# Last 64 tokens as one high|low operand, a 256-key first score tile, and a moved weight split

## The chip, the cores and the metric

The kernel runs on one core of one Trainium2 chip. The metric is the device time of one execution in microseconds; the kernel before takes 835.9 us, the median of 3 runs (834.54 to 836.42). Five engines work in parallel: TensorE (PE, matmuls; PEld is its loading of the stationary operand), VectorE (DVE), ScalarE (ACT), GpSimd (POOL) and SyncE (SP, which issues DMAs here).

## What is computed

For each of 8 batches of 576 tokens and 8 heads of 64:

```python
def sm_attn(qq, kk, vv):                       # softmax attention
    ...
p_packed = sm_attn(p, k, v)                    # 32 packed queries
out = sm_attn(q, p_packed, p_packed)           # 576 tokens over 32 packed keys
...
h = gelu_tanh(x @ w_in)                        # 512 -> 1024
u, v = h[..., :512], h[..., 512:]
v_n = (v - mu) / sqrt(var + 1e-06) * g_ln      # norm over 512 features
v_s = einsum('ts,bsd->btd', w_sg, v_n) + b_sg  # mixing of tokens
x = x + (u * v_s) @ w_out
...
logits = x @ w_gate                            # 4 experts, the best 2 weighted by softmax
for e in range(E):                             # causal attention of head size 64 each
    ye = causal_attn(x @ wq[e], x @ wk[e], x @ wv[e]) @ wo[e]
    out += weight[e] * ye
```

## The kernel before

**Precision.** Each float32 product is three matmuls of a reduced-precision format (fp32r): every operand is split in a high part and a low part (the remainder), and the passes are high·high, high·low and low·high (`PASSES`; names end in h and l, as gh, gl, a2h, a2l, vnh, vnl). ScalarE usually makes the high part by a copy into fp32r, and VectorE or POOL the low part by a subtraction.

**Tokens.** 576 tokens are five tiles, 4 of 128 and one of 64 (`TOK`, tile c = 4). `VT` groups them as (0,1), (2,3), (4,). Operands that are stationary for tile 4 have 128 columns in v (a2 is stored 640 wide, with its last 64 columns repeated) and 64 columns in vlog.

**One batch b.** (1) Packed attention: pp, the 32 packed keys and values; s (L392), the tokens' scores against them, turned into weights bt and a2f; their split a2h/a2l (`a2_split`). (2) W' = ppT·w_in (wp, L605), copied and split into wph (ScalarE, L621) and wpl (VectorE, L85). (3) `front`: v = a2·W' (`v_mm`, L667), gelu (`v_gelu`, L672), norm (`v_stats` L677 to L681, `v_pow` on POOL, `v_scale` L689, `v_high` L695 and L697 on ScalarE, `v_low` L704 to L708 on VectorE), which gives vnh and vnl of each token tile; u in four tiles of 128 features (`u_tile`, L748). (4) vs = w_sg·vn in four column tiles m (`vs_mm`, L778 for token tiles 0 to 3 in order, six matmuls each, then L782 and L784 for tile 4); the gate g = u·vs and its split (`gate_high`, `gate_low`). (5) qk (L834 from the gate, L846 from the packed attention) and vlog (L877, L881), which makes the values v2 and the 4 gate logits lg; `gates` makes the expert weights. (6) Causal attention of the batch, by steps with one letter and a number: S, the scores sc of a query tile j (0 to 4) and a head pair pr, with mask, maximum nm, exp and sums (`att_exp`, L930 to L940; where matmuls are named apart they are S and the rest E; number 2j + pr, so E1 is query tile 0, pair 1, and E3 query tile 1, pair 1); N, the division by the sums (L946 to L949); T, transposes; y and o, values and output product.

**Order.** TensorE and SP run in the order of the program's text. The attention of batch b, the packed attention of batch b+1 and the transposing loads of batch b+2 (kx and qx, by DMA through DRAM copies turned_k and turned_q, one step per `tick`) are interleaved by hand, in `later_back` and `back`; batch 0's start has a written order (`ORDER`). The order on VectorE, ScalarE and POOL is laid down by a scheduler when the program is built, apart from stretches marked `manual_schedule`. So a change of the text can move steps of these engines far from it.

**w_o.** `prep_w_o` (L347) loads each half of the output weight (wst, by SP), makes its high part on ScalarE (L82) and its low part on POOL (L85). It is called at the end of `first_back`, ahead of the first steps of batch 2.

**PSUM.** Products go to one tag of four buffers (`pd`); the slots of tag A in SBUF hold the gate's parts, two column tiles in one slot of 1152.

## Time and profile before

| | |
|---|---|
| Median of 3 runs | 835.9 us (834.54 to 836.42) |
| The profiled execution | 836.55 us, its span 834.8 us |
| Mean granted TensorE clock | 0.994 |
| TensorE busy | 802.2 us, 96%, 7523 matmuls |
| VectorE busy | 571.7 us, 68% |
| ScalarE busy | 429.1 us, 51% |
| POOL busy | 228.0 us, 27% |
| Chain that ended last | TensorE 81%, VectorE 8%, DMA 6%, ScalarE 2% |

The span is the time from the first to the last recorded instruction; the execution's own time is a little longer. The chain is followed back from the last instruction, at each step to what released it. A matmul's duration in the trace is its time through the array, and matmuls overlap: the pace of a row of them is read from their starts. Times are in us from the span's start. In brackets behind a row of a timeline stands the engine's idle time before it and what ended it. The step from batch to batch is 94.1 us in the middle of the span.

### The profile page before, as it was taken

To read this page: it belongs to the slowest core of one execution; us is meant where nothing else is said; L and a number is where in the kernel's file an instruction comes from. 1 tells how busy PE (TensorE), PEld (TensorE's weight loads), DVE (VectorE), ACT (ScalarE), POOL (GpSimd) and SP (SyncE) were. 2 spreads that over 40 slices of the span, in tenths; PEclk is the share of its full clock that TensorE was granted. 3 is DMA by queue.
4 is the path that set the end of the run, shared out by engine and by line. 5 is a ranking of instruction groups with operands and counts; after the bars stand their busy time and mean duration, and the time that the engine had idled before them with its cause. 6 is when DMAs were issued, how large, how long until landed. Compare 5 with 4: busy or idle time off the path is not lost.

```text
span 834.8 us, 19249 instructions
## 1 busy us (share of the span) xinstructions
PE 802.2 (96%) x7523; PEld 693.3 (83%) x7523; DVE 571.7 (68%) x1359; ACT 429.1 (51%) x983; POOL 228.0 (27%) x301
## 2 busy tenths in 40 slices
...
GB/s 253 288 186 170 230 268 133 174 50 220 147 154 108 107 224 113 177 43 222 142 163 107 103 227 113 161 58 217 147 155 116 98 232 8 77 14 27 20 2 58
DMA packets 172710, 115.00 MB, mean 138 GB/s; under 512 B 119306, under 2 KB 153610, under 8 KB 169804
## 3 DMA queue, kind: packets, MB, share of 16 engines
...
q10 hardware_dynamic: 6976, 1.58, 0.9%
...
HBM read 69.18 MB, written 29.63 MB: 118 GB/s over the span
## 4 chain that ended last, share of the span: by engine, by line
PE 81%; DVE 8%; DMA 6%; ACT 2%; issue 1%; SPq 1%; ACTq 0%; POOL 0%; DVEq 0%; POOLq 0%
PE vs L778 11%; PE qk L834 11%; PE y L1017 7%; PE vlog L877 6%; PE qk L846 6%; PE v L667 6%; PE u L748 5%; PE o L1066 5%; PE sc L930 4%; PE aTp L988 4%; PE vlog L881 3%; PE s L392 2%; PE sc L961 2%; PE aTp L1002 1%; DVE wpl L85 1%
## 5 line engine op out<-in xcount | busy, mean ns | idle before, releaser
L473 POOL COPY kT<-kp 128x576 uint16<-128x576 uint16 x56 | 50.8, 984 | 159.3 <-DMA kp<-turned_k 135.1
L778 PE MATMUL vs<-w_sg,vnh 128*128 128x288 f32 x512 | 91.6, 301 | 1.5 <-ACT vs L82 1.5
L834 PE MATMUL qk<-gh,w_qk 128*128 128x288 f32 x512 | 90.6, 299 | 0.0
L940 ACT ACTIVATE at<-sc,nm 128x256 f32<-128x256 f32 (+3 forms) x128 | 66.1, 525 | 37.9 <-DVE nm L934 34.3
L834 PEld LDWEIGHTS qk<-gh,w_qk 128*128 128x128 f32 x512 | 74.7, 188 | 9.7 <-issue 8.8
L778 PEld LDWEIGHTS vs<-w_sg,vnh 128*128 128x128 f32 x512 | 74.5, 188 | 8.3 <-issue 3.9
L82 ACT ACTIVATE aT<-aTp 128x512 f32<-128x512 f32 (+4 forms) x160 | 59.3, 437 | 18.4 <-PE aTp L988 13.3
...
L685 POOL TENSOR_TENSOR rstd<-rstd,mhalf 128x1 f32<-128x1 f32 x40 | 36.5, 917 | 88.5 <-DVE rstd L681 88.0
L877 PE MATMUL vlog<-w_vg,gh 128*128 128x260 f32 (+1 forms) x320 | 60.5, 287 | 0.0
L473 POOL COPY qT<-qp 128x576 uint16<-128x576 uint16 x56 | 43.0, 837 | 59.8 <-DMA qp<-turned_q 59.6
L1017 PE MATMUL y<-aT,v 128*64 128x128 f32 (+2 forms) x960 | 58.3, 263 | 1.0 <-ACT aT L82 0.9
L1017 PEld LDWEIGHTS y<-aT,v 128*64 128x64 f32 (+1 forms) x960 | 46.8, 136 | 13.3 <-issue 5.8
L949 DVE TENSOR_SCALAR at<-at,sm,gw 128x256 f32<-128x256 f32 (+3 forms) x128 | 54.9, 471 | 1.6
L778 PE MATMUL vs<-w_sg,vnl 128*128 128x288 f32 x256 | 54.8, 296 | 0.9 <-POOL vnl L85 0.9
L834 PE MATMUL qk<-gl,w_qk 128*128 128x288 f32 x256 | 54.8, 296 | 0.5 <-DVE gl L85 0.5
L934 DVE TENSOR_REDUCE nm<-sc 128x2 f32<-128x256 f32 (+3 forms) x64 | 51.3, 820 | 1.2
L877 PEld LDWEIGHTS vlog<-w_vg,gh 128*128 128x128 f32 (+1 forms) x320 | 47.1, 178 | 4.0 <-DVE lg L886 2.8
L1066 PE MATMUL o<-w_o,y 128*128 128x512 f32 x186 | 50.0, 403 | 0.0
L846 PE MATMUL qk<-a2h,bdq 128*128 128x288 f32 x256 | 45.9, 301 | 0.0
L877 PE MATMUL vlog<-w_vg,gl 128*128 128x260 f32 (+1 forms) x160 | 45.1, 282 | 0.0
L988 PE MATMUL aTp<-ident,at 128*128 128x128 f32 x320 | 43.3, 274 | 0.0
...
## 6 DMA issues: line engine op xcount, KB each, us to landing
...
```

The costliest lines, as they stand in the source:

```text
L82: nc.scalar.activation(o, i, AF.Copy, scale=scale)
L473: nc.gpsimd.tensor_copy(w[:, i], t[:, i].rearrange("p h n -> p (h n)"))
L778: nc.tensor.matmul(pt[:, h, :], s["vn", c][x][:, cols], w_sg[y][:, c, hs(h)], start=(c, x, y) == (0, 0, 0), stop=False)
L834: nc.tensor.matmul(o[:, h, :], W["w_qk"][y][:, m, cols], s["g", m][x][:, hs(h)], start=first and (m, x, y) == (0, 0, 0), stop=not first an ...
L846: nc.tensor.matmul(o[:, h, :], s["bd", Q][y][:, cols], s["a2", Q][x][:, hs(h)], start=first and (Q, x, y) == (0, 0, 0), stop=not first and ...
L877: nc.tensor.matmul(pt[:n, ci, :260], s["g", m][x][:, c * P:c * P + n], W["w_vg"][y][:, m, :], start=(m, x, y) == (0, 0, 0), stop=False)
L934: nc.vector.tensor_reduce(nm, pt[:, :, :L], axis=AX.X, op=OP.max, negate=True)
L940: nc.scalar.activation(ats[e][:, :L], pt[:, e, :L], AF.Exp, bias=nm[:, e:e + 1], accum_out=sm[:, e:e + 1])
L949: nc.vector.tensor_scalar(ats[e][:, :L], ats[e][:, :L], sm[:, e:e + 1], s["w"][:, j, 2 * pr + e:2 * pr + e + 1], op0=OP.mult, op1=OP.mult)
L988: nc.tensor.transpose(pt[:, e, c * P:c * P + P], ats[e][:, c * P:c * P + P], ident)
L1017: nc.tensor.matmul(pt[64 * e:64 * e + 64, pr * w:pr * w + w], s["v2"][:m, c, col:col + D], s["aT", pr, e, j][c][:m, :], start=c == 0, stop ...
L1066: nc.tensor.matmul(pt, ys[:, pr, x, :], W["w_o"][y][:, pr, :], start=i == 0, stop=i == 5)
```

## The change

Four things are changed.

1. For the last 64 tokens, high and low parts lie side by side as one stationary operand of 128 columns: in a2h (whose columns 576 to 639 now hold the low part of the last 64), and in the gate, where each column tile has a slot of its own, [high 576 | copy of the low part's last 64 | low 576]; the copy is `gate_beside`, four POOL copies a batch. `v_mm` of tile 4 then has four matmuls (2 passes by 2 halves Q) in place of six, and `vlog` of tile 4 twelve in place of 18. Rows 64 to 127 of the product hold the low parts' contributions, which are added: in `v_gelu` by a ScalarE copy and a VectorE addition ahead of the gelu, in `vlog` by a copy and an addition each for v2 and lg, and POOL copies lg to the upper rows. The low·low product comes in with it. The norm of tile 4 works on 64 partitions.
2. `front` computes tile 4 first, then tiles 0, 1, then 2, 3.
3. The first score tile (query tile 0) multiplies with 256 keys in place of 128; the second 128 are not read.
4. `prep_w_o` moves from the end of `first_back` to `back(0)`, behind qk(b, 1), keep_last_q and a tick.

Also `cmp` and `eq` of the gates share the tag "rem". The diff, cut to its core:

```diff
-        for o, i0, n in ((0, 0, S), (S, 512, 64)):
-            act_copy(hi[:, o:o + n], f[:, i0:i0 + n])
-            lo_part(nc.gpsimd, lo[:, o:o + n], f[:, i0:i0 + n], hi[:, o:o + n])
+        act_copy(hi[:, :S], f)
+        lo_part(nc.gpsimd, lo[:, :S], f, hi[:, :S])
+        lo_part(nc.gpsimd, hi[:, S:], f[:, 512:], hi[:, 512:S])
...
     def v_mm(b, pt, c):
         s = ST[b]
         n = 0
+        if c == 4:
+            for y in range(2):
+                for Q in range(2):
+                    nc.tensor.matmul(pt, s["a2", Q][0][:, 512:640], wp_part(b, 1, y, Q), start=n == 0, stop=n == 3)
+                    n += 1
+            return
         for x, y in PASSES:
             for Q in range(2):
                 nc.tensor.matmul(pt, s["a2", Q][x][:, c * P:(c + 1) * P], wp_part(b, 1, y, Q), start=n == 0, stop=n == 5)
                 n += 1
 
     def v_gelu(b, pt, c):
-        vg = ST[b]["vg", c] = slot("t", w=512, name="vg")
+        vg = slot("t", w=512, name="vg")
+        if c == 4:
+            vg = vg[:64]
+            act_copy(vg, pt[64:])
+            nc.vector.tensor_tensor(vg, vg, pt[:64], op=OP.add)
+            pt = vg
+        ST[b]["vg", c] = vg
         nc.scalar.activation(vg, pt, AF.Gelu_apprx_tanh)
...
     def v_high(b, c):
         s = ST[b]
         hi, lo = s["vn", c] = (slot("B", F32R, 512, name="vnh"), slot("B", F32R, 512, name="vnl"))
         vg, rstd = s["vg", c], s["rstd", c]
-        nc.scalar.activation(hi, vg, AF.Copy, scale=rstd)
+        nc.scalar.activation(hi[:TOK[c]], vg, AF.Copy, scale=rstd)
         if c == 4:
-            nc.scalar.activation(lo[:64], vg[:64], AF.Copy, scale=rstd[:64])
+            nc.scalar.activation(lo[:64], vg, AF.Copy, scale=rstd)
...
     def v_low(b, c):
...
         else:
-            nc.vector.scalar_tensor_tensor(hi[64:P], vg[64:P], rstd[64:P], hi[64:P].bitcast(F32),
-                                           op0=OP.mult, op1=OP.subtract)
+            nc.vector.scalar_tensor_tensor(hi[64:], vg, rstd, hi[:64].bitcast(F32), op0=OP.mult, op1=OP.subtract)
             nc.vector.memset(lo[64:P].bitcast(F32), 1.0)
...
     def gate_high(b, m):
         s = ST[b]
-        if ("gt2", m // 2) not in s:
-            s["gt2", m // 2] = (slot("A", F32R, name="gh"), slot("A", F32R, name="gl"))
-        a = (m % 2) * S
-        s["g", m] = [t[:, a:a + S] for t in s["gt2", m // 2]]
+        t = s["gx", m] = slot("A", F32R, name="g")
+        s["g", m] = [t[:, :S], t[:, S + 64:]]
...
+    def gate_beside(b):
+        for m in range(4):
+            t = ST[b]["gx", m]
+            nc.gpsimd.tensor_copy(t[:, S:S + 64], t[:, 2 * S:])
...
         pt = pd("vlog")
         for ci, c in enumerate(cs):
+            if n < P:
+                i = 0
+                for y in range(2):
+                    for m in range(4):
+                        nc.tensor.matmul(pt[:, 0, :260], s["gx", m][:, 512:640], W["w_vg"][y][:, m, :], start=i == 0,
+                                         stop=False)
+                        i += 1
+                    for Q in range(2):
+                        nc.tensor.matmul(pt[:, 0, :260], s["a2", Q][0][:, 512:640], s["bdv", Q][y], start=False,
+                                         stop=(y, Q) == (1, 1))
+                continue
             for m in range(4):
                 for x, y in PASSES:
-                    nc.tensor.matmul(pt[:n, ci, :260], s["g", m][x][:, c * P:c * P + n], W["w_vg"][y][:, m, :],
+                    nc.tensor.matmul(pt[:, ci, :260], s["g", m][x][:, c * P:c * P + P], W["w_vg"][y][:, m, :],
                                      start=(m, x, y) == (0, 0, 0), stop=False)
             for Q in range(2):
                 for x, y in PASSES:
-                    nc.tensor.matmul(pt[:n, ci, :260], s["a2", Q][x][:, c * P:c * P + n], s["bdv", Q][y],
+                    nc.tensor.matmul(pt[:, ci, :260], s["a2", Q][x][:, c * P:c * P + P], s["bdv", Q][y],
                                      start=False, stop=(Q, x, y) == (1, 1, 0))
-        nc.scalar.activation(s["v2"][:n, cs[0]:cs[0] + k, :], pt[:n, :k, :256], AF.Copy)
-
-        for o in range(0, P, n):
-            nc.vector.tensor_copy(s["lg"][o:o + n, cs[0]:cs[0] + k, :], pt[:n, :k, 256:260])
+        if n < P:
+            v4, l4 = s["v2"][:n, 4, :], s["lg"][:, 4, :]
+            nc.scalar.activation(v4, pt[n:, 0, :256], AF.Copy)
+            nc.vector.tensor_tensor(v4, v4, pt[:n, 0, :256], op=OP.add)
+            nc.vector.tensor_copy(l4[:n], pt[n:, 0, 256:260])
+            nc.vector.tensor_tensor(l4[:n], l4[:n], pt[:n, 0, 256:260], op=OP.add)
+            nc.gpsimd.tensor_copy(l4[n:], l4[:n])
+            return
+        nc.scalar.activation(s["v2"][:, cs[0]:cs[0] + k, :], pt[:, :k, :256], AF.Copy)
+        nc.vector.tensor_copy(s["lg"][:, cs[0]:cs[0] + k, :], pt[:, :k, 256:260])
...
         L = j * P + P
+        n = max(L, 2 * P)
         qs, ks = s["qk", pr], s["qk", 2 + pr]
         pt = pd("sc")
         for i, (x, y) in enumerate(PASSES):
             for e in range(2):
                 r = slice(64 * e, 64 * e + 64)
-                nc.tensor.matmul(pt[:, e, :L], qs[x][r, j * P:L], ks[y][r, :L], start=i == 0, stop=i == 2)
+                nc.tensor.matmul(pt[:, e, :n], qs[x][r, j * P:L], ks[y][r, :n], start=i == 0, stop=i == 2)
         nc.vector.tensor_tensor(pt[:, :, j * P:L], pt[:, :, j * P:L],
...
     def front(b, go):
 
-        for cs in VT:
+        for cs in (VT[2], VT[0], VT[1]):
             v_tiles(b, cs)
             tick()
...
         keep_last_q(b, 0)
+        gate_beside(b)
         do_all("p0 Q0 p1 Q1")
         vlog(b, VT[2])
         do_all("P0 P1")
         vlog(b, VT[1])
         do_all("r")
-        for j in range(2):
-            prep_w_o(j)
         ahead(b + 2)
...
         qk(b, 1)
         keep_last_q(b, 1)
         tick()
+        if b == 0:
+            for j in range(2):
+                prep_w_o(j)
         nxt("E0 E2")
```

How the change moves instructions is shown at three places, with the operations as the built programs have them (the numbers behind a name tell buffers apart; line numbers after the change are those of the new file).

**ScalarE, from the front's last steps to the first exps of the attention, batch 1 (batches 2 to 7 read the same).** vnh is the high part of a token tile's normed v, 64x512 for tile 4, vnl 64x512 the high part's copy for its second operand; at<-sc is an exp. Before:

```order
L695 ACTIVATE vnh<-vg,rstd 128x512
L755 ACTIVATE u<-u 128x576
L695 ACTIVATE vnh<-vg,rstd 128x512
L755 ACTIVATE u<-u 128x576
L695 ACTIVATE vnh<-vg,rstd 128x512
L697 ACTIVATE vnl<-vg,rstd 64x512
L940 ACT_TABLE_LOAD
L940 ACTIVATE at,sm_2004<-sc,nm_2002 128x128 x2
L940 ACTIVATE at,sm_2022<-sc,nm_2020 128x256 x2
```

Now:

```order
L709 ACTIVATE vnh<-vg,rstd 128x512
L768 ACTIVATE u<-u 128x576
L709 ACTIVATE vnh<-vg,rstd 128x512
L684 ACTIVATE vg<-v 128x512
L768 ACTIVATE u<-u 128x576
L709 ACTIVATE vnh<-vg,rstd 128x512
L768 ACTIVATE u<-u 128x576
L973 ACT_TABLE_LOAD
L973 ACTIVATE at,sm_2000<-sc,nm_1998 128x128 x2
L709 ACTIVATE vnh<-vg,rstd 128x512
L973 ACTIVATE at,sm_2018<-sc,nm_2016 128x256 x2
```

Before, the five tiles' vnh all stand ahead of the table load. Now the last 128x512 vnh, that of tile 3, stands behind the load and the two exps of E1.

**VectorE, the same place.** causal is the mask's addition to a score tile, nm the row maximum (E1's first, then E3's), vnl<-vg,rstd,vnh a low part. Before:

```order
L681 TENSOR_SCALAR rstd<-mv 128x1
L689 SCALAR_TENSOR_TENSOR vg<-vg,mv,g_bc 128x512
L704 SCALAR_TENSOR_TENSOR vnl<-vg,rstd,vnh 128x512
L931 TENSOR_TENSOR sc<-sc,causal 128x2x128
L708 MEMSET vnl 64x512
L931 TENSOR_TENSOR sc<-sc,causal 128x2x128
L706 SCALAR_TENSOR_TENSOR vnh<-vg,rstd,vnh 64x512
L934 TENSOR_REDUCE nm_2002<-sc 128x2
L934 TENSOR_REDUCE nm_2020<-sc 128x2
L946 TENSOR_SCALAR sm_2004<-sm_2004 128x2
```

Now:

```order
L718 SCALAR_TENSOR_TENSOR vnl<-vg,rstd,vnh 128x512
L964 TENSOR_TENSOR sc<-sc,causal 128x2x128
L692 BN_AGGR mv<-bnst 128x2
L964 TENSOR_TENSOR sc<-sc,causal 128x2x128
L967 TENSOR_REDUCE nm_1998<-sc 128x2
L694 TENSOR_SCALAR rstd<-mv 128x1
L702 SCALAR_TENSOR_TENSOR vg<-vg,mv,g_bc 128x512
L967 TENSOR_REDUCE nm_2016<-sc 128x2
L979 TENSOR_SCALAR sm_2000<-sm_2000 128x2
L980 RECIPROCAL sm_2000<-sm_2000 128x2
L718 SCALAR_TENSOR_TENSOR vnl<-vg,rstd,vnh 128x512
L982 TENSOR_SCALAR at<-at,sm_2000,gw 128x128 x2
```

Before, both nm stand behind every step of the norm. Now rstd and scale of tile 3 stand between them, and its vnl behind both.

**SP, the end of batch 0.** Before:

```order
L196 DMA w_in_1338<-kept_in_110 128x2048
L351 DMA wst_1563<-in_moe_wo_dram 128x512
L351 DMA wst_1567<-in_moe_wo_dram 128x512
L438 DMA pn<-in_p_dram 128x2x64 x2
L455 DMA_TRANSPOSE kx<-in_k_dram 128x1152
L460 DMA turned_k_1682<-kx 128x1152
L455 DMA_TRANSPOSE kx<-in_k_dram 128x1152
```

Now:

```order
L196 DMA w_in_1336<-kept_in_110 128x2048
L438 DMA pn<-in_p_dram 128x2x64 x2
L455 DMA_TRANSPOSE kx<-in_k_dram 128x1152
L460 DMA turned_k_1668<-kx 128x1152
L455 DMA_TRANSPOSE kx<-in_k_dram 128x1152
L351 DMA wst_1674<-in_moe_wo_dram 128x512
L351 DMA wst_1678<-in_moe_wo_dram 128x512
L460 DMA turned_k_1723<-kx 128x1152
```

The two wst loads, w_o's halves, have moved behind pn, one kx, its turned_k and a second kx. On ScalarE, the split of w_o (L82) stood ahead of the copies of the first vlog (64x256), of ppT and of the second vlog. Now it stands behind them and ahead of the two bt exps; POOL has its low parts ahead of its bt steps before and now:

```order
L868 ACTIVATE qk<-qk 128x576
L912 ACTIVATE v_1431<-vlog 64x256
L426 ACTIVATE ppT<-ppT 128x128 x2
L918 ACTIVATE v_1431<-vlog 128x512
L82 ACTIVATE w_o_1672<-wst_1674 128x512
L82 ACTIVATE w_o_1672<-wst_1678 128x512
L527 ACTIVATE bt<-bt 128x576 x2
L918 ACTIVATE v_1431<-vlog 128x512
```

In this row of ScalarE only w_o's place has moved.

## Rows read from the trace of the kernel before

**Rows 1.** The page: span, and TensorE's busy time, share and instructions.

```profile
span 834.8 us, 19249 instructions
...
PE 802.2 (96%) x7523; PEld 693.3 (83%) x7523; DVE 571.7 (68%) x1359; ACT 429.1 (51%) x983; POOL 228.0 (27%) x301
```

**Rows 2.** The chain of waits, 330 to 362 us: start, us, what.

```profile
339.13 6.66 PE v L667 x28
...
352.47 0.89 PE sc L930 x12
353.36 3.38 PE vs L778 x24
```

**Rows 3.** The chain of waits, 400 to 425 us: vlog of tile 4, then of tiles 2, 3.

```profile
413.36 1.58 PE vlog L877 x12
...
415.65 1.45 PE vlog L877 x12
```

**Rows 4.** The instructions of vlog, 407 to 421 us: ns min/median/max, place, forms.

```profile
L877 PEld LDWEIGHTS vlog<-w_vg,gh x40: 133/188/192, 407.7 to 418.7; 128*128 128x128 f32 x32, 128*64 128x64 f32 x8
```

**Rows 5.** TensorE's groups by form, sc: count | busy us, mean ns | idle before.

```profile
L930 PE MATMUL sc<-qk 64*128 64x384 f32 x96 | 10.8, 353 | 0.0
L930 PE MATMUL sc<-qk 64*128 64x256 f32 x96 | 9.2, 297 | 0.7 <-ACT at L967 0.7
L930 PE MATMUL sc<-qk 64*128 64x128 f32 x96 | 8.8, 289 | 0.0
```

**Rows 6.** VectorE's timeline: start, us, operation [idle before <-releaser].

```profile
343.70 1.29 DVE L677 BATCH_NORM_STATS2 bnst<-vg 128x6 f32<-128x512 f32 x2 [1.45 <-ACT vg L672]
...
353.33 0.74 DVE L704 SCALAR_TENSOR_TENSOR vnl<-vg,rstd,vnh 128x512 fp32r<-128x512 f32 x1
353.99 0.42 DVE L931 TENSOR_TENSOR sc<-sc,causal 128x256 f32<-128x256 f32 x1
...
355.42 0.75 DVE L706 SCALAR_TENSOR_TENSOR vnh<-vg,rstd,vnh 64x512 fp32r<-64x512 f32 x1
356.20 1.02 DVE L934 TENSOR_REDUCE nm<-sc 128x2 f32<-128x256 f32 x2
```

**Rows 7.** ScalarE's timeline, the same place.

```profile
353.85 0.72 ACT L695 ACTIVATE vnh<-vg,rstd 128x512 fp32r<-128x512 f32 x1 [0.19 <-POOL rstd L685]
...
356.70 1.28 ACT L940 ACT_TABLE_LOAD   x1 [1.51 <-DVE nm L934]
358.00 0.37 ACT L940 ACTIVATE at<-sc,nm 128x128 f32<-128x128 f32 x1
```

**Rows 8.** SP's timeline, the end of batch 0.

```profile
117.38 2.57 SPq L196 DMA_DIRECT2D w_in<-kept_in  x2
...
124.09 5.12 SPq L455 DMA_TRANSPOSE kx<-in_k_dram  x1
132.14 0.36 SPq L460 DMA_DIRECT2D turned_k<-kx  x1
132.60 2.08 SPq L455 DMA_TRANSPOSE kx<-in_k_dram  x1
```

**Rows 9.** The chain of waits, 118 to 154 us.

```profile
122.34 8.26 DMA wst<-in_moe_wo_dram
```

**Rows 10.** POOL's timeline, the end of batch 0.

```profile
130.65 2.50 POOL L85 TENSOR_TENSOR w_o<-wst,w_o 128x512 fp32r<-128x512 f32 x2 [3.85 <-DMA wst<-in_moe_wo_dram]
134.50 1.16 POOL L526 TENSOR_TENSOR bt<-bt,mx 128x576 f32<-128x576 f32 x1 [1.36 <-DVE mx L525]
```

**Rows 11.** VectorE's timeline, the end of batch 0.

```profile
149.67 1.23 DVE L85 TENSOR_TENSOR wpl<-wp,wph 128x1024 fp32r<-128x1024 f32 x1 [2.36 <-ACT wph L621]
```

**Rows 12.** TensorE's timeline, the end of batch 0.

```profile
131.83 1.21 PE L392 MATMUL s<-qT,ppT 64*32 64x288 f32 x32 [1.83 <-ACT ppT L426]
```

**Rows 13.** Busy us (x) in stretches, PE PEld DVE ACT POOL, PEclk, DMA share, GB/s.

```profile
30.00:34.00 4.00, 1.28 (x22) 0.62 (x20) 3.93 (x7) 3.22 (x5) 1.27 (x1) 0.95 1.05 395
34.00:38.00 4.00, 3.61 (x5) 1.58 (x6) 3.40 (x7) 1.22 (x2) 1.03 (x1) 0.50 1.09 304
```

More of the change, by code (lines that the diff above doesn't have):

```diff
@@ L675, in v_stats @@
         s = ST[b]
-        st = small.tile([P, 6], F32, name="bnst")
+        n = TOK[c]
+        st = small.tile([P, 6], F32, name="bnst")[:n]
         nc.vector.bn_stats(st, s["vg", c])
-        mv = s["mv", c] = small.tile([P, 2], F32, name="mv")
+        mv = s["mv", c] = small.tile([P, 2], F32, name="mv")[:n]
         nc.vector.bn_aggr(mv, st)
-        rstd = s["rstd", c] = small.tile([P, 1], F32, name="rstd")
+        rstd = s["rstd", c] = small.tile([P, 1], F32, name="rstd")[:n]
         nc.vector.tensor_scalar(rstd, mv[:, 1:2], LN_EPS, None, op0=OP.add)
@@ L684, in v_pow @@
         rstd = ST[b]["rstd", c]
-        nc.gpsimd.tensor_tensor(rstd, rstd, mhalf, op=OP.pow)
+        nc.gpsimd.tensor_tensor(rstd, rstd, mhalf[:TOK[c]], op=OP.pow)
     def v_scale(b, c):
         s = ST[b]
-        nc.vector.scalar_tensor_tensor(s["vg", c], s["vg", c], s.pop(("mv", c))[:, 0:1], g_bc, op0=OP.subtract, op1=OP.mult)
+        nc.vector.scalar_tensor_tensor(s["vg", c], s["vg", c], s.pop(("mv", c))[:, 0:1], g_bc[:TOK[c]],
+                                       op0=OP.subtract, op1=OP.mult)
     def v_high(b, c):
@@ L714, in v_high_0 @@
         nc.scalar.activation(vg, vg, AF.Copy, scale=s.pop(("rstd", c)))
-        act_copy(hi, vg)
+        act_copy(hi[:TOK[c]], vg)
         if c == 4:
-            act_copy(lo[:64], vg[:64])
+            act_copy(lo[:64], vg)
     def v_low_0(b, c):
@@ L725, in v_low_0 @@
         else:
-            lo_part(nc.gpsimd, hi[64:P], vg[64:P], hi[64:P])
+            lo_part(nc.gpsimd, hi[64:], vg, hi[:64])
             nc.gpsimd.memset(lo[64:P].bitcast(F32), 1.0)
@@ L893, in gates @@
         mine = lg[:, :, :, None].to_broadcast(T4)
-        cmp = small.tile(T4, F32, name="cmp", bufs=1)
-        eq = small.tile(T4, F32, name="eq", bufs=1)
+        cmp, eq = [small.tile([P, 2 * D], F32, tag="rem", name=n, bufs=2)[:, :NT * E * E].rearrange("p (c i j) -> p c i j", c=NT, i=E) for n in ("cmp", "eq")]
         nc.vector.tensor_tensor(cmp, other, mine, op=OP.is_gt)
@@ L1170, in later_back @@
         keep_last_q(b, 0)
+        gate_beside(b)
         qk_gated(b, 2, True)
```

15 lines of the change are left out of this document (7 added, 8 removed).

## Prediction, made before the result was known

> **What bounds the kernel now.** I read the page first: TensorE is busy for 802.2 us of a span of 834.8 us [rows 1], so the end moves only by what changes TensorE's own work, or by waits that are put into its row. The profiled execution took 836.55 us; the sum below is made against that, and the median of the runs is 0.65 us lower. Next I read the chain of waits in a steady stretch. Batches repeat there, and between 339 and 361 us, which is the front of a batch, the chain is TensorE alone: v's matmuls from the third on, 28 in 6.66 us, u, 12 of sc (score tiles E1 and E3), then 24 of vs, the spatial gating's first column tile, in 3.38 us [rows 2]. So TensorE waits for nothing here, and a wait that appears here is paid in full, seven times, once for each of batches 1 to 7 (batch 0 has its own written order). Then I read what VectorE and ScalarE do in the same stretch, since they make what vs reads, and last the end of batch 0, which is where w_o's load is moved.
>
> **TensorE's work.** A v matmul takes 6.66/28 = 0.238 us [rows 2]; the last tile has 4 in place of 6, which saves 0.47 us. The last tile's vlog runs from 413.36 to the next tile's start at 415.65: 2.29 us for 18 matmuls. The next tile's 12 take 1.45 us with 128 stationary columns [rows 3], 0.121 each. Twelve of the wide kind in place of 18 narrow ones save at least 6 x 0.12 = 0.72 us and at most 2.29 - 1.45 = 0.84; I take 0.72, as the first matmuls of a tile also pay for the change of shape. That is 1.2 us a batch. The chance against it is the stationary load: 64 columns load in 133 ns and 128 in 188 ns [rows 4], so if the loads set the pace, 12 x 188 = 2.26 us against 18 x 133 = 2.39 us would save next to nothing. The steps of 0.121 and 0.127 us, both shorter than either load, say that loads run under the matmuls. The Trainium skill (TensorE: Matmul & The Clock Gate, section LDWEIGHTS) has the load's time proportional to its columns, 128/1.2 = 107 ns against 53; by it, as an estimate, 12 wide loads would take 1.28 us against 0.95, and vlog would lose time. The trace agrees on the direction, not on the ratio: 188 ns against 133.
>
> The first score tile gets 256 keys, 6 matmuls for each of 2 head pairs and 8 batches, 96 in all. By form, 128 keys take 289 ns and 256 take 297 [rows 5]: 96 x 8 ns = 0.8 us at most; two heads run beside each other, so half of that, 0.4. The upper end is the price of 128 more columns from 256 to 384, 353 - 297 = 56 ns, which is 2.7 us by the same halving. I take 0.4, whose rows are the very shapes.
>
> **The new order in front of vs.** ScalarE's order shows that the high part of tile 3 (vnh) now stands behind the exp table's load and the two exps of E1, and VectorE's order shows its rstd, scale and low part behind or between the row maxima. Before, all five tiles were finished ahead of the first maximum. When is tile 3 ready now?
> - VectorE begins its norm work at 343.70 and reaches E1's maximum (nm) at 356.20, almost without a pause [rows 6]. Two things bring that maximum forward. Tile 4 comes first: its four matmuls end some 1.4 us sooner than the first pair did, with a copy of about 0.6 us before its gelu, so the first statistics start about 1.1 us earlier (my estimate from the 0.46 us a pair of v matmuls takes). And tile 3's scale and low part (0.66 us each from start to start, as 353.33 to 353.99 [rows 6]), with its rstd, now come later: 1.4 us. So nm starts at about 356.20 - 1.1 - 1.4 = 353.7.
> - ScalarE waits for nm, loads the table at 356.70 and starts the first exp at 358.00 [rows 7]: 1.80 us behind nm's start. An exp of 128x128 takes 0.37 us [rows 7], two take 0.7. So 353.7 + 1.8 + 0.7 = 356.2 is where tile 3's vnh may begin; 0.72 us for it [rows 7], and it is there at 356.95.
> - TensorE starts vs at 353.36 - 0.47 (v is shorter), and reads tile 3 after 18 matmuls of 3.38/24 = 0.141 us: 352.9 + 2.5 = 355.4. It waits 1.55 us. Then the low part (0.74 us) is done at 357.7, and TensorE wants it 4 matmuls after 356.95, at 357.5: 0.2 more.
> - So 1.8 us a batch, 12.6 us over seven. The lower end: nm cannot start before E1's scores are there (half of the sc group's 0.89 us: 352.45) and both masks are added (0.40 each), some 353.3, which leaves 1.4; if the exps stood closer too, 0.9. The upper end: if norm operations of 64 partitions break the overlap of VectorE's steps (the 64-partition one starts 0.43 us after the mask before it [rows 6]) and nothing comes earlier, 2.5.
>
> ScalarE's two copies a batch (v and vlog of the last tile), VectorE's two adds, and POOL's four copies of low parts add about 1.2, 1.2 and 0.9 us. They stand where these engines wait for TensorE (ScalarE waits 1.51 us for nm alone [rows 7]); if that cover were gone, the cost would again be a wait of vs, and is inside the 2.5.
>
> **w_o's load, at the end of batch 0.** Before, its two DMAs go out on SP between w_in and the transposing load kx. They take 8.26 us to land [rows 9], and ScalarE's copy of them holds up ppT, for which TensorE waits 1.83 us before 131.83 [rows 12]. Moved, they stand on SP behind pn, kx, the store turned_k (which waits until kx has landed) and the next kx. Without them SP could go on from the end of w_in, 117.38 + 2.57 = 119.95; with the 1.2 us of pn between, the first kx goes out at 121.2 in place of 124.09, 2.9 us earlier. turned_k, before at 132.14, then comes at 129.3; the second kx takes 2.08 us [rows 8]; w_o goes out between 131.8 and 132.6. It lands 1.3 us later at best (133.9), 7.2 at worst (139.8, as slow as before); I take 136, since the big loads ahead of it (two w_in, one kx) have then landed. ScalarE's order has both halves of w_o ahead of the bt exps, and POOL's has its low parts (2.50 us for two) ahead of both bt steps [rows 10]. POOL's first bt step, before at 134.50, then starts at 136 + 0.7 + 2.5 = 139.2: 4.7 us later. From there a chain without gaps leads by bt, sums and a2f to the gates, E0's mask and exps, wph and wpl, which v of batch 1 needs. Its slack is the 2.36 us that VectorE waits before wpl [rows 11]. TensorE would lose about 2 to 3 us there, and with it what batch 0 saved (1.2) and the 1.8 us wait it no longer has before. Against the sum in which only batches 1 to 7 save, I put +3; the ends are -3 (landing at 133.9: the old wait and batch 0's saving are won) and +6.
>
> **The sum.** 7 x -1.2 = -8.4; score tile +0.4; vs +12.6; w_o +3: together +7.6 us, 844.1 for the profiled execution and 843.5 against the median. As the lower part of 0.9 to 2.5 is the better founded, I say **843.0**.
>
> **The rivals.**
> - *vs waits, w_o does not* (w_o lands by 134): -8.4 + 0.4 + 12.6 - 1.2 - 1.8 = +1.6, 837.5 against the median. For it: the 8.26 us were taken behind two w_in loads and beside kx. Against it: SP's own order, which cannot issue it before 131.8.
> - *The clock falls too.* A wait of some 4 us of TensorE before v of batch 1. Between 34 and 38 us, after a stretch in which TensorE was busy for 1.28 of 4 us, the granted clock is 0.50, its lower level of 1.2 GHz [rows 13]; that is some 1.7 us of work lost. With w_o at its upper end this is +7.6 + 3 + 1.7 = +12.3, about 848.
> - *w_o as forecast, no wait at vs*: -8.4 + 0.4 + 3 = -5.0, 831.
> - *The other side: faster.* Tile 3's parts are ready when vs wants them. The point that decides is E1's first maximum: if ScalarE is released by nm at 352.0 or before, vnh is done by 355.4. Then with w_o harmless the sum is -8.4 + 0.4 - 1.2 - 1.8 = -11, **825**. Against it: E1's scores are themselves only finished at about 352.47 + 0.45 - 0.47 = 352.45, and both masks go ahead of the maximum.
> - *Wide loads set the pace*, so that vlog saves nothing: 8 x 0.72 = 5.8 us more, 849. Against it: the steps of [rows 3]. The page named above speaks for it.
>
> **How the numbers follow.** My forecast, 839 to 846, has a chance of 0.48; vs alone (837.5) 0.16; the clock too (848) 0.12; w_o alone (831) 0.08; neither (825) 0.11; wide loads (849) 0.05. A measurement of this kernel tells about 0.2%, 1.7 us, from no change. Slower by more: 0.48 + 0.12 + 0.05 and a third of the second case, 0.70. Faster: 0.08 + 0.11 and a little of the second, 0.20. Same: 0.10. The range of 831 to 849 leaves out the case of 825, part of 831 and the end beyond 849, not quite 2 in 10. The likeliest one's own range is 839 to 846.
>
> **What would show it.** In the profile after: the vs matmuls of tile 3 with an idle time of 1 to 2 us put down to ScalarE's vnh, seven times; ScalarE's vnh right behind E1's exps; a v group that is 16 matmuls smaller and a vlog group 48 smaller, at unchanged steps; w_o's landing near 136 us and TensorE idle before v of batch 1; no more wait for ppT. If TensorE runs through tile 3 of vs without a pause, the forecast is wrong, and the time should be near 825 or 831.

## The result and the profile after

The changed kernel takes 845.6 us, the median of 4 runs (845.5 to 849.13), where before takes 835.22 (4 runs beside it): the ratio is 1.0135, with a 95% interval of 1.0103 to 1.0167. It is slower by 10.4 us of median. The profiled executions, 845.5 against 836.55 us, differ by 9.0 us, and so do their spans.

The page of the kernel after, against [rows 1]:

```profile
span 843.8 us, 19236 instructions
...
PE 800.4 (95%) x7459; PEld 689.2 (82%) x7459; DVE 568.9 (67%) x1375; ACT 431.4 (51%) x975; POOL 231.6 (27%) x341
```

TensorE has 64 fewer matmuls and is busy for 1.8 us less (its busy time holds the stretches at half clock that are read below), and the span is 9.0 us longer. The waits of TensorE say where that stands (what waited, on what: us in total, times, longest):

```profile
PE vs L791 <- ACT vnh L709: 11.4, 7, 1.6
...
PE qk L857 <- DVE lg L919: 2.3, 1, 2.3
```

Neither row exists before. The first is one wait in each of batches 1 to 7, the second stands at the end of batch 0. The three timelines of the batch that [rows 2, 6, 7] show (shifted by some 1.9 us, the distance that has added up until there) have the first wait in full. ScalarE:

```profile
352.37 0.59 ACT L684 ACTIVATE vg<-v 128x512 f32<-128x512 f32 x1
...
356.23 1.28 ACT L973 ACT_TABLE_LOAD   x1 [1.38 <-issue]
357.53 0.37 ACT L973 ACTIVATE at<-sc,nm 128x128 f32<-128x128 f32 x1
...
357.88 0.36 ACT L973 ACTIVATE at<-sc,nm 128x128 f32<-128x128 f32 x1
...
358.23 0.72 ACT L709 ACTIVATE vnh<-vg,rstd 128x512 fp32r<-128x512 f32 x1
```

VectorE:

```profile
344.40 0.69 DVE L690 BATCH_NORM_STATS2 bnst<-vg 64x6 f32<-64x512 f32 x1 [0.20 <-ACT vg L684]
...
349.47 0.48 DVE L721 MEMSET vnl<- 64x512 f32 x1 [0.16 <-issue]
...
353.73 0.69 DVE L690 BATCH_NORM_STATS2 bnst<-vg 128x6 f32<-128x512 f32 x1
...
355.01 0.43 DVE L964 TENSOR_TENSOR sc<-sc,causal 128x256 f32<-128x256 f32 x1
...
355.75 0.41 DVE L967 TENSOR_REDUCE nm<-sc 128x2 f32<-128x256 f32 x1
356.08 0.15 DVE L694 TENSOR_SCALAR rstd<-mv 128x1 f32<-128x1 f32 x1
356.14 0.74 DVE L702 SCALAR_TENSOR_TENSOR vg<-vg,mv,g_bc 128x512 f32<-128x512 f32 x1
...
358.98 0.75 DVE L718 SCALAR_TENSOR_TENSOR vnl<-vg,rstd,vnh 128x512 fp32r<-128x512 f32 x1 [0.24 <-ACT vnh L709]
```

TensorE:

```profile
354.73 0.79 PE L791 MATMUL vs<-w_sg,vnh 128*128 128x288 f32 x4
...
356.96 0.42 PE L791 MATMUL vs<-w_sg,vnl 128*128 128x288 f32 x2
359.00 0.79 PE L791 MATMUL vs<-w_sg,vnh 128*128 128x288 f32 x4 [1.62 <-ACT vnh L709]
359.78 0.53 PE L791 MATMUL vs<-w_sg,vnl 128*128 128x288 f32 x2
```

The reader follows it from row to row: tile 3's gelu stands on ScalarE at 352.37, its statistics on VectorE at 353.73; the masks are added from 355.01 on, E1's maximum is taken at 355.75, the table load follows at 356.23, the exps end at 358.23, and only then does ScalarE make tile 3's vnh. TensorE had come to it 1.62 us before 359.00. The low part starts at 358.98 and takes 0.75 us, so the pair that reads it starts 0.78 us after the four matmuls on vnh, where an undisturbed pair starts 0.53 after. The 1.62 us are counted from the end of the matmuls before; from start to start the pause is 1.78 us (356.96 to 359.00, less the 0.26 that an undisturbed pair takes).

The matmuls of both kernels come in the same groups, so each group's start can be set beside its twin's. In the shown batch the distance changes at four places: -0.47 us over v, +2.13 over the first tile of vs, -0.65 over tile 4's vlog, and +0.02 at a wider score group. Of the seven vs steps six are 2.13 to 2.17 us and one is 3.69, in batch 5. There TensorE's granted clock fell behind the wait, to 0.50, the lower level of 1.2 GHz; the stretches (busy us, PEclk, DMA share, GB/s) read:

```profile
548.00:549.00 1.00, 0.00 (x0) 0.00 (x0) 0.17 (x1) 1.00 (x5) 0.00 (x0) 1.00 0.99 284
...
551.00:553.00 2.00, 2.00 (x10) 2.00 (x9) 1.48 (x3) 0.15 (x1) 0.00 (x0) 0.50 0.38 147
...
555.00:557.00 2.00, 2.00 (x18) 1.95 (x16) 0.43 (x1) 0.21 (x2) 0.00 (x0) 1.00 0.00 0
```

The end of batch 0 is the second wait. The chain of waits there, against [rows 9 to 11]:

```profile
128.36 3.86 DMA wst<-in_moe_wo_dram
132.24 0.64 ACT w_o L82
133.01 2.54 POOL w_o L85 x2
135.55 1.13 POOL bt L526
...
149.27 1.24 DVE wpl L85
150.55 0.73 PE v L668 x2
```

and TensorE at the wait, with the granted clock around it:

```profile
141.05 1.33 PE L857 MATMUL qk<-a2h,bdq 128*128 128x288 f32 x4 [2.28 <-DVE lg L919]
```

```profile
140.00:142.00 2.00, 0.95 (x4) 0.95 (x5) 2.00 (x11) 0.10 (x1) 0.00 (x0) 0.66 0.00 0
142.00:144.00 2.00, 2.00 (x10) 2.00 (x10) 1.84 (x6) 1.23 (x3) 0.47 (x2) 0.50 0.00 0
144.00:146.00 2.00, 2.00 (x17) 2.00 (x16) 1.93 (x8) 0.16 (x1) 0.42 (x2) 0.99 0.00 0
```

w_o lands at 132.2 us, and its low parts hold back POOL's first bt step to 135.5: that is 26.1 us after the first matmul of bdq (109.4), where before it came 23.0 us after (134.5 and 111.5). The chain behind it is late with it. TensorE stands still for 2.28 us, and its clock is at 0.50, 1.2 GHz, for the 2 us from 142 on.

### The profile page after: what moved, and what is told of

The parts are those of the page before. It is cut to its first block, busy times and chain, and to the rows that moved or that the text cites. A ratio compares the mean times of both kernels' runs of the same rounds, so it can differ in the third digit from the quotient of the medians.

```text
span 843.8 us, 19236 instructions
## 1 busy us (share of the span) xinstructions
PE 800.4 (95%) x7459; PEld 689.2 (82%) x7459; DVE 568.9 (67%) x1375; ACT 431.4 (51%) x975; POOL 231.6 (27%) x341
## 4 chain that ended last, share of the span: by engine, by line
PE 69%; DVE 16%; ACT 6%; DMA 4%; issue 3%; SPq 1%; POOL 0%; ACTq 0%; DVEq 0%; POOLq 0%
PE qk L845 11%; PE vs L791 10%; PE y L1050 6%; PE qk L857 6%; PE o L1099 5%; PE vlog L904 5%; PE aTp L1021 4%; PE sc L963 4%; DVE bnst L690 3%; DVE vg L702 3%; PE vlog L908 3%; PE s L392 2%; PE sc L994 2%; DVE vnl L718 1%; PE aTp L1035 1%
## 5 line engine op out<-in xcount | busy, mean ns | idle before, releaser
L845 PEld LDWEIGHTS qk<-g,w_qk 128*128 128x128 f32 x768 | 103.9, 189 | 10.6 <-issue 8.8
L845 PE MATMUL qk<-g,w_qk 128*128 128x288 f32 x768 | 110.6, 298 | 0.6 <-DVE g L85 0.3
L82 ACT ACTIVATE aT<-aTp 128x512 f32<-128x512 f32 (+4 forms) x160 | 59.2, 435 | 27.6 <-PE aTp L1021 22.5
L698 POOL TENSOR_TENSOR rstd<-rstd,mhalf 128x1 f32<-128x1 f32 (+1 forms) x40 | 36.9, 929 | 96.6 <-DVE rstd L694 96.6
L880 POOL CAST g<-g 128x64 fp32r<-128x64 f32 x32 | 8.5, 270 | 181.4 <-DVE g L85 121.2
L982 DVE TENSOR_SCALAR at<-at,sm,gw 128x256 f32<-128x256 f32 (+3 forms) x128 | 51.1, 440 | 1.8
L904 PE MATMUL vlog<-w_vg,g 128*128 128x260 f32 x384 | 52.0, 285 | 0.0
L904 PEld LDWEIGHTS vlog<-w_vg,g 128*128 128x128 f32 x384 | 48.4, 189 | 0.8 <-PE s L392 0.5
L473 POOL COPY kT<-kp 128x576 uint16<-128x576 uint16 x56 | 45.4, 888 | 10.3 <-DMA kp<-turned_k 10.3
L857 PEld LDWEIGHTS qk<-a2h,bdq 128*128 128x128 f32 x256 | 38.1, 193 | 6.6 <-issue 3.2
L1021 PE MATMUL aTp<-ident,at 128*128 128x128 f32 x320 | 43.3, 274 | 0.0
```

The source lines that it names most:

```text
L82: nc.scalar.activation(o, i, AF.Copy, scale=scale)
L473: nc.gpsimd.tensor_copy(w[:, i], t[:, i].rearrange("p h n -> p (h n)"))
L845: nc.tensor.matmul(o[:, h, :], W["w_qk"][y][:, m, cols], s["g", m][x][:, hs(h)], start=first and (m, x, y) == (0, 0, 0), stop=not first an ...
L857: nc.tensor.matmul(o[:, h, :], s["bd", Q][y][:, cols], s["a2", Q][x][:, hs(h)], start=first and (Q, x, y) == (0, 0, 0), stop=not first and ...
L904: nc.tensor.matmul(pt[:, ci, :260], s["g", m][x][:, c * P:c * P + P], W["w_vg"][y][:, m, :], start=(m, x, y) == (0, 0, 0), stop=False)
L982: nc.vector.tensor_scalar(ats[e][:, :L], ats[e][:, :L], sm[:, e:e + 1], s["w"][:, j, 2 * pr + e:2 * pr + e + 1], op0=OP.mult, op1=OP.mult)
```

## The experiments

All are compared with the kernel before on the same chip. Startup differs from execution to execution even of equal code (the first bdq of batch 0 starts between 109.2 and 115.7 us in the 14 profiles), so beside the medians two stretches of the profiled executions are read: from that bdq (its first matmul) to u of batch 1, the end of batch 0; and from there to the last matmul, batches 1 to 7.

| kernel | median us (before) | ratio, 95% interval | end of batch 0 | batches 1 to 7 |
|---|---|---|---|---|
| before | | | 45.9 | 674.3 |
| after | 845.6 (835.2) | 1.0135 (1.0103 to 1.0167) | 47.2 | 684.2 |
| x1 order alone | 836.5 (836.6) | 1.0004 (0.9985 to 1.0024) | 44.0 | 674.2 |
| x2 narrow score | 846.5 (836.6) | 1.012 (1.0095 to 1.0144) | 47.2 | 683.9 |
| x3 w_o back | 844.7 (836.6) | 1.009 (1.0058 to 1.0121) | 43.3 | 684.3 |
| x4 high part first | 840.1 (836.6) | 1.0036 (1.0017 to 1.0055) | 47.3 | 676.4 |
| x5 norm first | 844.5 (835.5) | 1.0105 (1.0079 to 1.013) | 45.8 | 680.8 |
| x6 vlog alone | 832.6 (835.5) | 0.9963 (0.9946 to 0.9979) | 43.4 | 670.5 |
| x7 old order | 852.1 (835.5) | 1.0204 (1.018 to 1.023) | 47.1 | 689.5 |
| x8 laid out | 826.5 (836.2) | 0.9882 (0.9865 to 0.99) | 43.5 | 667.2 |
| x9 memset on POOL | 832.3 (836.2) | 0.9952 (0.9934 to 0.997) | 49.1 | 669.6 |
| x10 all three | 827.6 (836.2) | 0.9897 (0.9879 to 0.9914) | 43.1 | 669.4 |
| x11 memset before | 836.1 (836.4) | 1.0 (0.9986 to 1.0014) | 44.0 | 674.5 |
| x12 w_o before | 840.9 (836.4) | 1.0059 (1.004 to 1.0078) | 48.4 | 674.4 |

**x1: the order of the tiles alone, in the kernel before.**

```diff
-        for cs in VT:
+        for cs in (VT[2], VT[0], VT[1]):
```

> The kernel before with one edit: the front computes tile 4 first, then 0, 1, then 2, 3. ScalarE's order keeps tile 3's high part ahead of the table load, VectorE's puts its low part behind E1's maximum. Theory (the wait of vs comes from tile 3's high part standing behind E1's exps, which needs the merged tile's copy and addition as well): within 2 us of before, 834 to 838, and no wait for vnh at tile 3 of vs. Rival (the order of the tiles alone makes tile 3 late): a wait of 1 us or more at vs in each of seven batches, 843 or more.

No difference, in the medians or in batches 1 to 7, and no wait at vs. The order of the tiles alone is not the cause.

**x2: the first score tile at 128 keys again.**

```diff
-        n = max(L, 2 * P)
+        n = L
```

> The changed kernel with the first score tile at 128 keys again. Theory: the wider tile costs 0.02 us per tile (two score groups a batch stepped by 0.02 us each in the trace after), so 845 to 846, the wait at vs unchanged at 1.6 us seven times. Rival (the wider tile makes E1's scores late and with them the whole row to vnh): the wait at vs shrinks by 0.3 us or more a batch and the time falls by 2 us or more.

Batches 1 to 7 shrink by 0.3 us, as 14 groups of 0.02 make; the median lies within the runs of the changed kernel. The wider tile is as good as free, and the wait at vs is not its doing.

**x3: the split of w_o where it was.**

```diff
+        for j in range(2):
+            prep_w_o(j)
         ahead(b + 2)
...
-        if b == 0:
-            for j in range(2):
-                prep_w_o(j)
         nxt("E0 E2")
```

> The changed kernel with the split of w_o called at the end of batch 0's first part again. Theory (the move of w_o gains about what it loses): TensorE waits for ppT again (1.8 us) and no longer 2.3 us for lg, and the clock does not fall there; wp of batch 1 starts within 1.5 us of the changed kernel's, time 844 to 847.5. Rival (the move cost 3 us, as in the sum of the prediction): 842.5 or less.

The theory written here falls in its own terms. The median fits it (844.7), but wp of batch 1 comes 3.5 us earlier after bdq, and the end of batch 0 takes 43.3 us where it took 47.2: by the stretch, the move costs 3.9 us. Nor does the old wait for ppT come back in full; it is 0.40 us here. In the profiled execution bdq starts 3.1 us later than in the changed kernel's (112.5 and 109.4), which hides the gain in its time; whether that holds for the other runs is not recorded. x12, and x9 beside x10, bear on it below.

**x4: tile 3's high part ahead of E1's exps.** Nothing else moves in ScalarE's row; on VectorE only the low part comes ahead of E1's sums.

```diff
             for f in (v_stats, v_pow, v_scale, v_high, v_low):
-                f(b, c)
+                if c != 3 or f not in (v_high, v_low):
+                    f(b, c)
...
-        go("S1 S3")
+        with tc.manual_schedule(engines={ET.Activation}):
+            v_high(b, 3)
+            v_low(b, 3)
+            go("S1 S3")
```

> The changed kernel with one row of ScalarE's order fixed: tile 3's high part goes ahead of the table load and E1's exps; all else stands. Theory: vnh of tile 3 is done about 357.6 where vs wants it at 357.4 (times of the batch shown for the changed kernel), its low part wants 0.2 us more, so 1.7 of the 2.1 us go, in seven batches 12 us, and with them the batch in which the clock fell (1.5 us): 831 to 834, faster than before. Rival (the wait is VectorE's late norm, so it only passes from vnh to vnl or to the transposes of E1): 841 or more.

Between the two: 0.8 to 0.9 us of the 2.1 go in each batch, and the clock's 1.5 once; 7.8 us in batches 1 to 7. What the expectation left out stands in the same place of x4's trace, on ScalarE, VectorE and POOL:

```profile
358.42 0.72 ACT L709 ACTIVATE vnh<-vg,rstd 128x512 fp32r<-128x512 f32 x1 [2.47 <-POOL rstd L698]
359.15 1.28 ACT L974 ACT_TABLE_LOAD   x1
```

```profile
356.85 0.41 DVE L968 TENSOR_REDUCE nm<-sc 128x2 f32<-128x256 f32 x1
357.17 0.15 DVE L694 TENSOR_SCALAR rstd<-mv 128x1 f32<-128x1 f32 x1
```

```profile
357.49 0.90 POOL L698 TENSOR_TENSOR rstd<-rstd,mhalf 128x1 f32<-128x1 f32 x1 [2.84 <-DVE rstd L694]
```

vnh needs rstd and its power, and VectorE comes to rstd only behind E1's maximum: rstd is there at 357.32, its power, on POOL, at 358.39, and vnh starts at 358.42. So the place of vnh is some two fifths of what a batch loses, and VectorE's row the rest.

**x5: the whole norm of tile 3 ahead of E1, on both engines.** Against x4:

```diff
-                if c != 3 or f not in (v_high, v_low):
+                if c != 3 or f not in (v_scale, v_high, v_low):
...
-        with tc.manual_schedule(engines={ET.Activation}):
+        with tc.manual_schedule(engines={ET.Activation, ET.DVE}):
+            v_scale(b, 3)
```

> The changed kernel with tile 3's scale, high part and low part all ahead of E1's mask, maximum and exps, on VectorE and ScalarE; the run before this one had moved the high part alone and left 1.25 us of wait a batch, because rstd on VectorE and its power on POOL still stood behind the masks and the maximum. Theory: statistics end at 354.3 (the changed kernel's batch), rstd 355.1, power 356.2, high part 356.9, low part 357.65, where vs wants them at 357.4 and 357.9: no wait above 0.2 us at vs. E1's exps end at about 360.5 and its transposes want them, normed, at 362: no wait there. So the 2.1 us go in seven batches, and the clock's 1.5: 828 to 832. Rival (E1's chain, 2 us later, now makes the transposes wait as long): 838 or more.

The rival, nearly in full. Of the 2.1 us a batch 1.7 go at vs, but E1's table load starts later, and 1.5 come back behind it, at y and the next scores:

```profile
PE y L1051 <- DVE gt L815: 5.9, 7, 0.8
...
PE y L1051 <- ACT aT L82: 2.2, 8, 0.9
```

```profile
361.68 0.75 DVE L718 SCALAR_TENSOR_TENSOR vnl<-vg,rstd,vnh 128x512 fp32r<-128x512 f32 x1 [1.20 <-ACT vnh L709]
```

```profile
363.30 1.28 ACT L974 ACT_TABLE_LOAD   x1 [1.65 <-DVE nm L968]
```

The load waits for a maximum that VectorE took only after it had idled 1.2 us for vnh. Batches 1 to 7 gain 3.4 us, 1.5 of it the clock's. Putting one late thing ahead of another in a full row passes the wait on.

**x6: the merged vlog alone.** v, the order, the score tile and w_o are as before; tile 4 of v takes six matmuls of 64 stationary columns.

```diff
-        if c == 4:
...
-            return
         for x, y in PASSES:
             for Q in range(2):
-                nc.tensor.matmul(pt, s["a2", Q][x][:, c * P:(c + 1) * P], wp_part(b, 1, y, Q), start=n == 0, stop=n == 5)
+                nc.tensor.matmul(pt[:TOK[c]], s["a2", Q][x][:, c * P:c * P + TOK[c]], wp_part(b, 1, y, Q), start=n == 0, stop=n == 5)
...
-            act_copy(vg, pt[64:])
-            nc.vector.tensor_tensor(vg, vg, pt[:64], op=OP.add)
-            pt = vg
+            pt = pt[:64]
```

> The changed kernel with v, the order of the tiles, the first score tile and w_o as before: tile 4 of v takes six matmuls with 64 stationary columns and needs no copy and addition; what stays is the merged vlog, the 64-partition norm and the gate's layout. The orders have all five high parts ahead of E1's exps, as before. Theory (the merged vlog saves 0.65 us a batch and nothing else waits): no wait for vnh, 8 x 0.65 = 5 us off, 829.5 to 832.5 where before is at 835 to 836.6. Rival (the copies and additions behind vlog, or the norm on 64 partitions, cost what it saves): 835 or more.

Steps of -0.65 us in every batch, as the theory says, and no wait for vnh; about 0.1 us a batch comes back at vs. It is faster than before by 0.37% (0.21 to 0.54%): 2.9 us of median where 5 was expected, and 3.8 us in batches 1 to 7.

**x7: the changed kernel with tile 4 last again.**

```diff
-        for cs in (VT[2], VT[0], VT[1]):
+        for cs in VT:
```

> The changed kernel with the front's tiles in the old order, 0, 1, then 2, 3, then 4; the copy and addition for tile 4 stay. ScalarE's order now has tile 4's two high parts behind E1's exps. Theory (the copy and addition lengthen the last tile's chain by 1.3 us, so that the scheduler lays E1's exps ahead of whichever tile comes last): the wait passes to tile 4 in vs, 1.5 us or more a batch, 842 to 850. Rival (computing tile 4 first is the cause): no wait at vs, 832 or less.

Slower than the change itself, and the wait has passed to tile 4, whose vnh VectorE finishes:

```profile
PE vs L795 <- DVE vnh L720: 14.4, 7, 2.2
```

With x1 and x6 this tells the cause apart. The new order without the merged v (tile 4 in four matmuls) has no such wait (x1), nor has the merged vlog without it (x6); the merged v has one in either order. What it adds in front of vs is a copy on ScalarE and an addition on VectorE for tile 4; that it also brings vs 0.47 us forward is not told apart from them. With them and the memset on VectorE, whichever tile comes last, the scheduler lays E1's steps ahead of its end. In the changed kernel that is tile 3, and the two steps stand in the chain of tile 4, which comes first: they reach tile 3 through the rows of the engines.

**x9: the changed kernel with one memset moved to POOL.** The edit takes 0.64 us out of VectorE's row: the memset at 349.47 in the rows above, 0.48 us, and the 0.16 us before it.

```diff
-            nc.vector.memset(lo[64:P].bitcast(F32), 1.0)
+            nc.gpsimd.memset(lo[64:P].bitcast(F32), 1.0)
```

> The changed kernel with one edit: the memset of tile 4's vnl (0.48 us on VectorE, 0.64 from start to start with the gap before it) goes to POOL. With it the scheduler lays tile 3's rstd and scale ahead of the masks, its high part ahead of the table load, its low part behind both maxima. Theory (VectorE's row in front of vs, over its brim by the added work, is what set the wait): in the changed kernel's batch rstd at 354.5, power 355.5, high part 356.2, low part 357.5, wanted at 357.4 and 357.9; E1's exps where they were; no wait at vs, nor at y as with the whole norm put first. 14 us of wait and the clock's 1.5 go: 828 to 832. Rival (the memset on POOL holds up the powers there, and rstd takes its place): a wait of 0.5 us or more at vs, 835 or more.

The wait of vs goes: batches 1 to 7 take 14.6 us less than in the changed kernel, and the median is below before. Part of it is the rows that the scheduler then makes by itself: rstd and scale of tile 3 ahead of the masks, its high part ahead of the table load, and on ScalarE its gelu one high part earlier, 2.98 us ahead of vs where the changed kernel has 2.36:

```profile
349.96 0.58 ACT L684 ACTIVATE vg<-v 128x512 f32<-128x512 f32 x1
...
354.26 0.73 ACT L709 ACTIVATE vnh<-vg,rstd 128x512 fp32r<-128x512 f32 x1 [1.42 <-POOL rstd L698]
355.01 1.28 ACT L973 ACT_TABLE_LOAD   x1
```

```profile
352.94 0.79 PE L791 MATMUL vs<-w_sg,vnh 128*128 128x288 f32 x4
```

How much of the 14.6 us the 0.64 us give and how much these rows is not separated: a kernel with them and the memset left on VectorE was not made. x4 and x5 are the two other rows that were tried with it there. What is left is the end of batch 0:

```profile
PE qk L857 <- DVE lg L919: 3.3, 1, 3.3
```

**x8: the same row written by hand.** The memset is on POOL as in x9, the first score tile has 128 keys as in x2, and w_o's split stands as in x3. The score tiles' matmuls, mask, maximum and exps become functions of their own, tile 3's statistics two, called in this order on VectorE and ScalarE:

```diff
-        go("S1 S3")
+        with tc.manual_schedule(engines={ET.Activation, ET.DVE}):
+            v_var(b, 3)
+            v_pow(b, 3)
+            v_scale(b, 3)
+            p1 = att_scores(b - 1, 1, 0)
+            p3 = att_scores(b - 1, 1, 1)
+            att_mask(p1, 0)
+            n1 = att_max(p1, 0)
+            att_mask(p3, 1)
+            v_high(b, 3)
+            v_low(b, 3)
+            n3 = att_max(p3, 1)
+            ...
```

> The same, with the first score tile at 128 keys, w_o's split where it was, and the order written by hand: rstd, scale, E1's mask and maximum, E3's mask, low part, E3's maximum on VectorE; high part, table load, exps on ScalarE. Theory: v and vlog save 1.1 us a batch and no wait is left in batches 1 to 7, so 826.5 to 831 and the faster of this and the next by less than 1 us. Rival (the hand-written row delays E3 and its transposes): 833 or more.

**x10: the edits of x2, x3 and x9 together, with the scheduler's order.**

> The memset on POOL, the first score tile at 128 keys, and w_o's split where it was, with the scheduler's order. Theory: v 0.47 x 7, vlog 0.65 x 8 off, and no wait in batches 1 to 7: 8.5 us under before, 826.5 to 830; 3.3 us under the merged vlog alone. Rival (the copy and addition of v give back what its two matmuls save): equal to the merged vlog alone, 831 to 833.

Both are the fastest kernels of this case: x8 is 1.2% (1.0 to 1.35%) below before, x10 1.0% (0.9 to 1.2%). In x10 vnh is made at 349.16, ahead of the load, and E1's exps are not late:

```profile
349.16 0.72 ACT L709 ACTIVATE vnh<-vg,rstd 128x512 fp32r<-128x512 f32 x1 [1.74 <-POOL rstd L698]
349.90 1.28 ACT L973 ACT_TABLE_LOAD   x1
351.20 0.37 ACT L973 ACTIVATE at<-sc,nm 128x128 f32<-128x128 f32 x1
```

```profile
349.72 0.42 PE L791 MATMUL vs<-w_sg,vnl 128*128 128x288 f32 x2
349.98 0.76 PE L791 MATMUL vs<-w_sg,vnh 128*128 128x288 f32 x4
350.72 0.53 PE L791 MATMUL vs<-w_sg,vnl 128*128 128x288 f32 x2
```

TensorE goes from tile 2's low part to tile 3's high part without a pause (0.26 us from start to start), and only the low part, behind E3's maximum, still costs 0.2 to 0.3 us. x8 puts that ahead too, and its batches 1 to 7 are 2.2 us shorter. Beside the merged vlog alone (x6, batches 1 to 7) x8 gains the 3.3 us that x10's expectation names for v, and x10 itself 1.1.

**x11: the memset moved in the kernel before** (x9's edit there).

> The kernel before with the memset of vnl moved to POOL, nothing else. Theory (before, vs waits for nothing, so VectorE's row has room and the memset is free): within 1.5 us of before, same verdict. Rival (the memset's move is worth something by itself, and the gain of the three-part version is partly its own): 833 or less with the same startup.

Nothing, as expected: in the kernel before nothing in front of vs is late, and the memset's move is worth nothing by itself.

**x12: the split of w_o moved in the kernel before.**

```diff
-        for j in range(2):
-            prep_w_o(j)
         ahead(b + 2)
...
+        if b == 0:
+            for j in range(2):
+                prep_w_o(j)
         nxt("E0 E2")
```

> The kernel before with one edit: the split of w_o moved as in the change. Theory (the move frees ppT but puts w_o's halves ahead of the bt steps, so that the gates of batch 0 come late and TensorE waits 2 us or more for lg, with half the clock behind it): the wait for ppT (1.8 us) goes, a wait for lg of 2 to 3.5 us comes, and the stretch from bdq of batch 0 to u of batch 1, 45.9 us before, becomes 46.5 to 49.5; 836.5 to 840. Rival (the move only frees ppT): that stretch shrinks by 1.8 us, 833 to 835.

Slower by 4.6 us of median, 0.6% (0.4 to 0.8%); the end of batch 0 takes 48.4 us. The median is 0.9 us above what was expected. Its trace has the wait for lg and the slow clock behind it:

```profile
PE qk L846 <- DVE lg L886: 2.6, 1, 2.6
```

```profile
140.00:142.00 2.00, 0.04 (x2) 0.00 (x0) 1.90 (x5) 0.00 (x0) 0.00 (x0) 1.00 0.00 0
...
144.00:146.00 2.00, 2.00 (x11) 2.00 (x9) 1.65 (x10) 1.47 (x4) 0.46 (x2) 0.50 0.00 0
```

In the table the end of batch 0 takes 43.1 to 44.0 us in six kernels with the split where it was (45.9 in the profile of before, which has 1.83 us of wait for ppT [rows 12], where x3 has 0.40 and the other five none), and 45.8 to 49.1 in seven with it moved; x9 and x10, which differ in the split and the score tile, have 49.1 and 43.1.

## Why the prediction was right

843.0 was said for 845.6, and slower with a chance of 0.7. The main mechanism, a wait of vs for tile 3's high part behind E1's exps, is the one that the traces show. That the sum comes so near is in part luck, as its terms read one by one show:

- **v and vlog, -8.4.** Measured -0.44 to -0.47 and -0.65 a batch: -7.7 over seven. vlog was put at 0.72 from the matmul's pace. Tile 4's twelve wide matmuls take 1.56 us from start to start, 0.13 each, where the 18 narrow ones took 2.29, 0.127 each; over the whole group 0.65 is left of that. So the rival that wide loads set the pace falls, as [rows 3] had said. By the rule of the Trainium skill (TensorE: Matmul & The Clock Gate, section LDWEIGHTS), that a load's time goes with its columns, the wide loads are the longer ones. The trace agrees (188 ns against 133, [rows 4]). It costs next to nothing here: the matmuls step at 0.12 to 0.13 us, less than either load takes.
- **The score tile, +0.4.** 0.3 (x2).
- **vs, +12.6, 1.8 a batch.** Six batches lost 2.13 to 2.17, one 3.69: 16.6 in all. The working held in its main times. Set back by the 1.85 us by which the two batches stand apart (vs at 354.73, where 352.9 was said), the maximum came at 353.9 for 353.7 and vnh was begun at 356.4 for 356.2. The pause from start to start was 1.78 us for 1.55, as vnh came 0.2 later, and the low part cost 0.35 where 0.2 was said: 0.25 in front of its own pair and 0.1 behind it. No term had the clock's 1.5 us in one batch. One step does not follow as written: 1.4 us less a copy of 0.6 is not the 1.1 by which the statistics were to start earlier. They did start 1.15 earlier; first come four matmuls in place of twelve, and eight at 0.23 less the copy are 1.2. Why the scheduler laid tile 3 behind E1 the prediction did not ask; it read it off the orders. x9 takes the wait away, by the memset and the rows that come with its move.
- **w_o, +3.** The chain was the right one, from w_o's low parts by bt, sums and gates to wpl. Its size was not. In the two profiles the end of batch 0 grows by 1.3 us, not by 3. The +3 was net of 1.8 for the wait for ppT and 1.2 for batch 0's saving, so it put some 6 us on what the move costs TensorE; x3 beside the changed kernel shows 3.9. POOL's first bt step came 3.2 us later, counted from bdq, where 4.7 was said. w_o was issued at 128.36, not between 131.8 and 132.6: SP came to the first kx 2.0 us earlier than was said (119.16), as the start of this execution was earlier, and the rest is a shorter first kx (7.40 us from its issue to turned_k, where [rows 8] have 8.05) and a shorter issue of the second (1.24 us for 2.08). From there its transfer took 3.86 us, about what 136 had left for it, so it landed at 132.2. And TensorE stopped earlier in the chain than was said, at qk, behind lg's copy on VectorE; before v of batch 1 only 0.49 us were left. Against the kernels of before that lack the wait for ppT (x1, x11: 44.0) the growth is 3.2 us. That this meets the +3, which had counted on that wait, is luck.
- **The whole.** The spans are 9.0 us apart where 7.6 was said: 9.8 in batches 1 to 7 (vs 16.6, v and vlog -7.3 from u of batch 1 on, the rest from the score tiles and small steps), 1.3 at the end of batch 0, and 2.2 less at the start, which is no effect of the change that a run here shows: bdq of batch 0 starts at 109.4 us in the changed kernel and at 112.5 in x3, whose text parts from it only behind that. So vs was 4.0 us too small, w_o 1.7 too large, and the start gave 2.2 that no term had. The step from 843.5 down to 843.0 was the wrong way.

The clock rival, 0.12 at about 848, came true in part: half the clock for some 2 us at the end of batch 0, and once behind a wait of vs.
